# Batch 3's x through the array's quarters, and batch 2's x later in its output stage with the first two tiles of the next h side by side

## The chip, the cores and the metric

One core of a Trainium2 chip. The metric is the device time of the core in microseconds. The profile's span is about 1.9 us shorter than it in most executions.

## The reference

Linear attention for 8 batches and 8 heads, then a two-layer MLP with an exact Gelu:

```python
q_s = softmax(q, axis=-1)          # (8, 8, 576, 64)
k_s = softmax(k, axis=2)           # over the sequence
kv  = einsum('bhsd,bhse->bhde', k_s, v)
attn = einsum('bhsd,bhde->bhse', q_s, kv)
x = attn.transpose(0, 2, 1, 3).reshape(4608, 512)
h = x @ w_in                       # 512 x 2048
out = (0.5 * h * (1 + erf(h / sqrt(2)))) @ w_out
```

## The kernel before

The kernel treats 512 of the 576 rows of each batch as one chunk (`M`), and the 8 x 64 remaining rows as a ninth. For a chunk, the h stage (`h_phase`) makes 16 tiles of h with 4 matmuls each, and ScalarE puts Gelu on each; the output stage (`y_phase`) makes 4 tiles of the output with 16 matmuls each. The attention of the next batches is threaded into these two stages: functions are called after a given tile `t`, or after matmul `(j, t)` of the output stage.

x of a batch is made by four matmuls, one for each pair of heads, with a block-diagonal 128x128 of kv as weights (`x_step`), and a copy (the evacuation) takes each product out of PSUM. Half of each block is zeros. For batches from `QB` on, the two heads of every second pair are swapped, so that the four 64x64 blocks of two pairs fall on the four quarters of the array, and eight 64x64 matmuls take the place of four whole ones (`x_quad`). The swap is made in the exponentials, in four activations rather than one.

```python
QB = 4
...
def exp_heads(b, dst, src):
    if b < QB:
        nc.scalar.activation(out=dst, in_=src, func=AF.Exp)
        return
    for s, u in ((0, 0), (1, 1), (2, 3), (3, 2)):
        nc.scalar.activation(out=dst[:, s::4], in_=src[:, u::4], func=AF.Exp)
...
def x_quad(b, engs="vvvv"):
    st[b]["xT"] = attn_sb.tile([128, HP, M], BF16, tag="xT", name="xT")
    for hp in range(HP):
        pool, tag = (psum_a, "a") if hp < 2 else (psum_y, "y")   # psum_y: the output stage's
        st[b][f"x{hp}"] = pool.tile([128, M], FP32, tag=tag, name="ps")
    for half in range(2):
        for r in range(2):
            for i in range(2):
                hp = 2 * half + i
                pr = slice(r * 64, r * 64 + 64)
                c = slice((r ^ i) * 64, (r ^ i) * 64 + 64)
                nc.tensor.matmul(
                    st[b][f"x{hp}"][c, :], kvbd[b][pr, hp, c], st[b]["qT"][pr, :, hp, :],
                    start=True, stop=True,
                )
    for hp in range(HP):
        x_evac(b, hp, engs[hp])
...
def h_phase(c, ins, groups={}, pre={}):      # groups={0: 2}: tiles 0 and 1 side by side
    ...
        for dm in range(NDM):
            for ps, t in zip(pss, ts):
                nc.tensor.matmul(
                    ps, wi_bf[:, dm, t * 128:(t + 1) * 128], xT[:, dm, :],
                    start=(dm == 0), stop=(dm == NDM - 1),
                )
...
load(3)                                      # q, k, v of batch 3
exp_q(2, parts=2); exp_k(2); exp_q(3); exp_k(3)
table(AF.Gelu)
y_phase(1, {
    (0, 15): [lambda: norm_q(2, 0, 2)],
    (1, 1): [lambda: norm_q(2, 1, 2, nc.vector)],
    (1, 12): [lambda: kv_step(2, (0, 1))],
    (2, 2): [lambda: kv_step(2, (2, 3))],
    (1, 15): [lambda: xbar_step(2)],         # DMA transpose of q: qT
    (3, 3): [lambda: x_step(2, 0)],
    (3, 6): [lambda: x_step(2, 1)],
    (3, 9): [lambda: x_step(2, 2)],
    (3, 12): [lambda: x_step(2, 3)],
})
```

The softmax here doesn't subtract the row's maximum and nothing guards it: scores larger than these inputs give would overflow.

## Time and profile before

| | kernel before |
|---|---|
| time, first three runs | 287.24 us median (287.09 to 288.22) |
| span of the profiled execution | 286.5 us |
| TensorE / ScalarE / VectorE / GpSimd busy | 97 / 55 / 42 / 13% |
| "the stretch": start of batch 1's output stage to start of batch 2's h stage | 62.20 to 79.14: 16.94 us |
| batch 2's h stage | 79.14 to 94.95: 15.81 us |
| VectorE's last copy ends; the span ends | 283.17; 286.5 |

In the profile's lines PE is TensorE, DVE VectorE, ACT ScalarE, POOL GpSimd and SP SyncE; SPq and ACTq are the queues on which SyncE and ScalarE issue DMAs. L323 is a line of the kernel: L323 x as whole matmuls, L346 x as quarters, L376 h, L386 the output. A bracket gives the idle time before an instruction, and what ended it.

Read it from the top: TensorE bounds the kernel, and the two stages that the change touches follow each other on TensorE.

### The profile page before, as it was taken

The page shows a single profiled execution, that of the slowest core. Times are in us where ns is not written, and L with a number is a line of the kernel's source. Part 1 is how long each engine was busy: PE and PEld are TensorE (multiplying, and loading weights), DVE is VectorE, ACT ScalarE, POOL GpSimd, SP SyncE. Part 2 cuts the span into 40 slices and gives each one's busy share as a digit, 9 for nine tenths or more (in the row PEclk, how much of TensorE's full clock was granted, in tenths as well). Part 3 has the DMA queues.
Part 4 walks back from the last instruction along what each step waited for, and adds up shares of the span by engine and source line. Part 5 has one row for each costly group of instructions (what it writes and reads, how often), then busy time and mean ns, then how long its engine had stood idle before and what let it go on. Part 6 is the DMA issues. An engine that isn't in the chain of part 4 may idle for free.

```text
span 286.5 us, 3845 instructions
## 1 busy us (share of the span) xinstructions
PE 278.7 (97%) x1507; PEld 131.3 (46%) x1507; DVE 120.2 (42%) x240; ACT 157.1 (55%) x251; POOL 38.5 (13%) x34
## 2 busy tenths in 40 slices
PE   8989999999899999999999999999999999999994
PEld 3534454445345445444544454445444444444443
DVE  7564387128595555345422632363235112110012
ACT  5777684779355843685268625771665165017400
POOL 5730032002020050005000400041002200000000
PEclk9999999999999999999999999999999999999999
DMA  7999999999809929932995189716701600120033
GB/s 233 375 383 385 373 388 296 293 283 244 161 37 251 297 97 233 258 115 76 214 266 146 73 190 264 172 73 160 136 0 72 147 2 0 73 76 0 0 73 76
DMA packets 58465, 50.05 MB, mean 175 GB/s; under 512 B 26576, under 2 KB 48336, under 8 KB 58448
## 3 DMA queue, kind: packets, MB, share of 16 engines
q1 hardware_dynamic: 58288, 49.68, 62.4%
q8 instruction: 12, 0.20, 0.3%
q10 hardware_dynamic: 160, 0.13, 0.1%
q14 instruction: 5, 0.04, 0.0%
HBM read 36.70 MB, written 9.44 MB: 161 GB/s over the span
## 4 chain that ended last, share of the span: by engine, by line
PE 77%; DMA 15%; SPq 2%; DVE 2%; ACT 1%; issue 1%; POOL 0%; ACTq 0%
PE ps L376 39%; PE ps L386 33%; DMA f<-in_v_dram 7%; DMA f<-in_q_dram 4%; DMA w<-in_moe_w_in_dram 3%; DMA qT<-e 2%; PE ps L251 2%; SPq L108 1%; PE ps L408 1%; DVE qsum L241 1%; PE ps L323 1%; PE ps L346 1%; SPq L117 1%; ACT L145 0%; SPq L463 0%
## 5 line engine op out<-in xcount | busy, mean ns | idle before, releaser
L381 ACT ACTIVATE g<-ps 128x512 bf16<-128x512 f32 x144 | 85.7, 597 | 100.0 <-PE ps L376 100.0
L376 PE MATMUL ps<-xT,wi_bf 128*128 128x512 bf16 x576 | 129.9, 379 | 1.0 <-POOL wi_bf L452 0.8
L386 PE MATMUL ps<-wo_bf,g 128*128 128x512 bf16 x560 | 124.0, 379 | 0.0
L376 PEld LDWEIGHTS <-wi_bf 128*128 128x128 bf16 x576 | 55.2, 98 | 66.5 <-issue 2.4
L386 PEld LDWEIGHTS <-g 128*128 128x128 bf16 x560 | 54.6, 98 | 65.8 <-issue 1.0
L393 DVE COPY y_sb<-ps 128x512 f32<-128x512 f32 x35 | 23.8, 686 | 73.2 <-PE ps L386 73.0
L243 POOL TENSOR_TENSOR e<-e,recq 128x1024 bf16<-128x1024 bf16 (+1 forms) x10 | 27.5, 2758 | 176.8 <-DVE recq L242 94.5
L356 DVE CAST xT<-ps 128x512 bf16<-128x512 f32 x33 | 21.6, 687 | 34.7 <-PE ps L346 20.8
L241 DVE TENSOR_REDUCE qsum<-e 128x16 f32<-128x1024 bf16 (+1 forms) x13 | 21.1, 1623 | 6.9 <-ACT e L145 6.7
L224 DVE CAST v_aug<-f 128x512 bf16<-128x512 f32 x24 | 10.3, 429 | 10.2 <-DMA f<-in_v_dram 9.6
L97 ACT ACT_TABLE_LOAD x9 | 11.5, 1283 | 0.9 <-PEq L659 0.7
L273 DVE TENSOR_SCALAR kvbd<-ps,rec 64x64 bf16<-64x64 f32 x48 | 11.6, 281 | 0.7
L476 PE MATMUL ps<-kvbd 128*128 128x512 bf16 x35 | 10.4, 467 | 1.2 <-DVE scr L85 1.2
L145 ACT ACTIVATE e<-f 128x1024 bf16<-128x1024 f32 (+1 forms) x7 | 8.1, 1174 | 4.9 <-DMA f<-in_q_dram 4.9
L182 ACT ACTIVATE ek<-f 64x1152 bf16<-64x1152 f32 x8 | 9.3, 1162 | 2.6 <-DMA f<-in_k_dram 2.5
L148 ACT ACTIVATE e<-f 128x512 bf16<-128x512 f32 x16 | 8.8, 618 | 0.0
L148 ACT ACTIVATE ek<-f 128x512 bf16<-128x512 f32 x16 | 8.7, 614 | 0.0
L251 PEld LDWEIGHTS <-ek 128*128 128x128 bf16 x96 | 6.8, 97 | 3.2 <-ACT ek L145 0.6
L251 PE MATMUL ps<-v_aug,ek 128*128 128x129 bf16 x96 | 8.1, 220 | 0.1
L467 DVE CAST wo_bf<-w 128x2048 bf16<-128x2048 f32 (+1 forms) x5 | 5.1, 1014 | 5.8 <-DMA w<-in_moe_w_out_dram 5.7
L323 PE MATMUL ps<-qT,kvbd 128*128 128x512 bf16 x16 | 6.1, 381 | 1.3 <-DMA qT<-e 0.7
L476 PEld LDWEIGHTS <-kvbd 128*128 128x128 bf16 x35 | 3.9, 116 | 6.7 <-issue 3.3
(53 smaller groups left out, 99.0 us busy)
## 6 DMA issues: line engine op xcount, KB each, us to landing
out_dram<-y_sb SPq DMA_DIRECT2D x32, 256.0 KB, 2.4
f<-in_q_dram SPq DMA_DIRECT2D x6, 1024.0 KB, 8.3
f<-in_k_dram SPq DMA_DIRECT2D x6, 1024.0 KB, 11.7
f<-in_v_dram SPq DMA_DIRECT2D x6, 1024.0 KB, 10.1
w<-in_moe_w_in_dram SPq DMA_DIRECT2D x6, 512.0 KB, 8.3
w<-in_moe_w_out_dram SPq DMA_DIRECT2D x3, 1024.0 KB, 12.1
f<-in_k_dram SPq DMA_DIRECT2D x4, 576.0 KB, 9.1
f<-in_v_dram SPq DMA_DIRECT2D x8, 288.0 KB, 9.4
```

The lines of the kernel that those rows point to most:

```text
L97: nc.scalar.activation(out=scr[:, 1:2], in_=scr[:, 0:1], func=func)
L148: nc.scalar.activation(out=dst[:, s::4], in_=src[:, u::4], func=AF.Exp)
L241: nc.vector.reduce_sum(out=qsum, in_=eq[:, :, hs, :], axis=AX.X)
L243: eng.tensor_tensor(out=eq[:, :, hs, :], in0=eq[:, :, hs, :], in1=recq.unsqueeze(3).to_broadcast([128, J, w, D]), op=ALU.mult,)
L251: nc.tensor.matmul(ps, st[b]["ek"][:, j, hs, :].rearrange("p h d -> p (h d)"), v_aug[b % 2][:, j, hp, 0:PW], start=(j == 0), stop=False,)
L273: nc.vector.tensor_scalar_mul(out=kvbd[b][pr, hps[i], c * 64:c * 64 + 64], in0=ps[pr, i, c * (D + 1):c * (D + 1) + D], scalar1=rec[pr, i:i ...
L356: nc.vector.tensor_copy(out=st[b]["xT"][:, hp, :], in_=ps)
L376: nc.tensor.matmul(ps, wi_bf[:, dm, t * 128:(t + 1) * 128], xT[:, dm, :], start=(dm == 0), stop=(dm == NDM - 1),)
L381: nc.scalar.activation(out=g[:, t, :], in_=ps, func=AF.Gelu)
L386: nc.tensor.matmul(ps, st[c]["g"][:, t, j * 128:(j + 1) * 128], wo_bf[:, t, :], start=(t == 0), stop=(t == NDF - 1),)
L393: nc.vector.tensor_copy(out=y_sb, in_=ps)
L476: nc.tensor.matmul(ps, zeros[:, 0:128], zeros, start=True, stop=True)
```

## The change

Its intent: keep TensorE from standing still for batch 2's transposed q (qT), with enough distance from x to h to hide x's last copy; and make batch 3's x at the price of two matmuls rather than four.

```diff
-    QB = 4
+    QB = 3
...  (exponentials of the ninth chunk: batch 3's heads swapped too, ten activations instead of five)
-        (3, 3): [lambda: x_step(2, 0)],
-        (3, 6): [lambda: x_step(2, 1)],
-        (3, 9): [lambda: x_step(2, 2)],
-        (3, 12): [lambda: x_step(2, 3)],
+        (3, 6): [lambda: x_step(2, 0)],
+        (3, 8): [lambda: x_step(2, 1)],
+        (3, 10): [lambda: x_step(2, 2)],
+        (3, 12): [lambda: x_step(2, 3, "s")],
...
         if QB <= b < B:
-            s[9] = [lambda: x_quad(b)]
+            s[12 if late else 9] = [lambda: x_quad(b)]
...
-        h_phase(c, ins)
+        h_phase(c, ins, groups={0: 2} if c == 2 else {})
```

`"s"` puts the last copy of x on ScalarE. `late` is true for batch 3.

More of the change, by code (lines that the diff above doesn't have):

```diff
@@ L157, in exp_main @@
             f = st[b][name + "f"]
-            nc.scalar.activation(out=e[:, 0:QB // 2], in_=f[:, 0:QB // 2], func=AF.Exp)
-            for s, u in ((0, 0), (1, 1), (2, 3), (3, 2)):
-                nc.scalar.activation(
-                    out=e[:, QB // 2:, s::4], in_=f[:, QB // 2:, u::4], func=AF.Exp
-                )
+            nc.scalar.activation(out=e[:, 0], in_=f[:, 0], func=AF.Exp)
+            exp_heads(2, e[0:R, 1], f[0:R, 1])
+            exp_heads(3, e[R:128, 1], f[R:128, 1])
+            exp_heads(4, e[:, 2:4].rearrange("p j h d -> p h j d"),
+                      f[:, 2:4].rearrange("p j h d -> p h j d"))
             return
```

## The prediction

> **What bounds the kernel now.** I read the page first: which engine is busy, then what it waits for.
>
> ```profile
> PE 278.7 (97%) x1507; PEld 131.3 (46%) x1507; DVE 120.2 (42%) x240; ACT 157.1 (55%) x251; POOL 38.5 (13%) x34
> ...
> PEclk9999999999999999999999999999999999999999
> ```
>
> TensorE is busy for 278.7 of 286.5 us, at full clock from end to end. No other engine passes 55%. Busy alone proves little here, so the second view is the list of what TensorE waited for over the whole span; this is all of it:
>
> ```profile
> engine line waited for: us in total, times, longest us
> PE ps L476 <- DVE scr L85: 1.2, 1, 1.2
> PE ps L376 <- POOL wi_bf L452: 0.8, 1, 0.8
> PE ps L323 <- DMA qT<-e: 0.7, 1, 0.7
> PE ps L197 <- DVE v_aug L188: 0.4, 1, 0.4
> PE ps L323 <- ACT kvbd L210: 0.3, 1, 0.3
> PE ps L323 <- DVE kvbd L212: 0.2, 1, 0.2
> ```
>
> Six waits, 3.6 us in all. Four of the six lie in the start-up or in batches 0 and 1 (their lines belong to the first two batches' own code), a fifth is the warm-up's. Only the third, 0.7 us for the transposed q (qT), lies where the change reaches. The reader should take from this that there are two ways to shorten the kernel: remove a TensorE wait, or give TensorE less to do. Shortening VectorE or ScalarE work cannot pay.
>
> The third view, TensorE's instructions in order of time, places that wait (start, duration, then the instructions of one kind in a row):
>
> ```profile
> 71.13 3.83 PE L386 MATMUL ps<-wo_bf,g 128*128 128x512 bf16 x17
> 75.69 0.38 PE L323 MATMUL ps<-qT,kvbd 128*128 128x512 bf16 x1 [0.73 <-DMA qT<-e]
> 75.91 0.81 PE L386 MATMUL ps<-wo_bf,g 128*128 128x512 bf16 x3
> ```
>
> This is batch 2's first x matmul, inside the last quarter of batch 1's output stage. TensorE is in order, so it stands from 74.96 to 75.69 us. The chain that ended last tells why qT comes then:
>
> ```profile
> 65.40 1.23 DVE qsum L241
> ...
> 68.90 1.24 DVE e L243
> ...
> 70.29 5.36 DMA qT<-e
> ...
> 75.69 0.38 PE ps L323
> ...
> 79.31 7.77 PE ps L376 x36
> ```
>
> The exponentials of q follow the last Gelu of the stage before (62.4 us), then come the row sums, the normalisation, and a DMA transpose of 5.36 us. Nothing in that chain waits for a TensorE instruction that the change moves, so qT stays at about 75.69 us. After this wait TensorE has none until the end.
>
> **What the Trainium skill says.** "Perfetto Trace Analysis", in Tensor Engine Instruction, says that a matmul's reported end is an estimate. The trace agrees: a 128x512 matmul is shown as 379 ns, yet 64 of them take 13.81 us on the chain, 0.2158 us each. I therefore count by starts. "TensorE: Matmul & The Clock Gate", in Back-to-back issue gap, gives N/2.4 + 2.5 ns, thus 216 ns for N = 512, which is this figure; the 131 ns which the same section gives for a stream of weight load and matmul pairs is not what this trace has. "TensorEngine Tiling (Array Packing)", in Key Properties, says that different tiles of the array run in parallel, and that changing the tiling mode drains it. Both are seen in the trace (next part). "Perfetto Trace Analysis", in DMA Instruction — HWDGE, says that the data movement is not in the DMA instruction's own window. So it is here: the transpose shows 3.34 us on its queue, and lands after 5.36 us.
>
> **The change, part by part.**
>
> *1. Batch 2's x moves from (3,3), (3,6), (3,9), (3,12) to (3,6), (3,8), (3,10), (3,12).* The instruction order confirms it: three more output matmuls come ahead of the first x, and two rather than three between the next. Nothing is added or removed on TensorE. It stopped at 74.96 us; three matmuls of 0.216 us take it to 75.61, where it meets qT at 75.69. So the wait falls from 0.73 to 0.08 us: 0.65 us gained, all of it on TensorE, which sets the end.
>
> *2. Its last evacuation goes to ScalarE, and the first two h tiles run side by side.* This is there to pay for part 1. From 75.69 us, four x matmuls and 9 output matmuls (three pairs and the last three) come before h: 13 x 0.216 = 2.81 us, so h would start at 78.50. Its start is shown at 79.14 before; the 0.64 us agrees with part 1 within rounding. The last x starts 4 matmuls earlier, at 77.64. An evacuation began 0.42 us after its matmul's start (75.69 to 76.11), so ScalarE starts at 78.06; the same copy took 0.586 us in batches 0 and 1, thus 78.65. In the new order its reader is the seventh matmul of h, at 78.50 + 6 x 0.216 = 79.80: 1.1 us to spare. Even without pairing, the fourth matmul would come at 79.15, with 0.5 us left. So I expect the pairing to remove no wait which would else be there: it is worth about zero. It also uses only two of the three PSUM buffers of h, and ScalarE's Gelu (597 ns a tile, against four matmuls or 0.86 us) catches up in a few tiles.
>
> *3. Batch 3's x: eight 64x64 matmuls rather than four 128x128.* Batches 4 to 7 already do this, so the cost is in the trace before:
>
> ```profile
> 118.32 0.38 PE L376 MATMUL ps<-xT,wi_bf 128*128 128x512 bf16 x1
> 118.63 0.41 PE L346 MATMUL ps<-qT,kvbd 64*64 64x512 bf16 x4
> 118.87 0.39 PE L346 MATMUL ps<-qT,kvbd 64*64 64x512 bf16 x4
> 119.19 0.39 PE L376 MATMUL ps<-xT,wi_bf 128*128 128x512 bf16 x1
> ```
>
> (These lines come from narrow looks at the same place; each is one row of four at a time, or one matmul.) Four start within some 0.02 us of each other, the next four 0.24 later. Entering the mode took 0.31 rather than 0.216 us, leaving it 0.32: the drains, some 0.1 us each. From the last h matmul ahead to the first behind it is 0.87 us. Four whole matmuls would have made that 5 x 0.216 = 1.08. The gain is 0.21 us, not the 0.43 that halving would give. A whole-stage check is independent of it: batch 2's h stage, with four whole matmuls, runs from 79.31 to 95.12 (15.81 us); the next, with the quarters, from 108.93 to 124.54 (15.61). Both hold the same 64 h matmuls and the same kv steps, and the difference is 0.20.
>
> *4. ScalarE pays for permuted heads.* q, k and k's rest of batch 3 are each four activations now. In batch 4's stage four 128x512 ones span 2.19 us for q and 2.17 for k, against 1.89 for one 128x2048; four 64x128 span 0.89 against 0.61. Together 0.30 + 0.28 + 0.28 = 0.86 us more. ScalarE finished at 74.27 before, and will at 75.1; it has nothing due until 78.06. For the last batch's q, about ten instructions in place of five (an estimate from the 0.3 us or so that each of the small ones takes, 1.32/4: 1.3 us more); its transpose starts at 224.36, lands some 4.7 us later (median) and is read at 234.2. Some 5 us are free. None of part 4 is on the path.
>
> Sum on the path: 0.65 + 0.21 + 0 + 0 = 0.86 us. 287.24 - 0.86 = 286.4 us, or 0.3%.
>
> **The rivals.**
>
> *A new wait for the PSUM buffers that the quarters borrow.* Two of the four x tiles come from the pool of the output stage, and here, unlike in batches 4 to 7, only three h tiles (12 matmuls, 2.59 us) are left behind them before that stage wants one back. In batch 4 VectorE began 0.45 us after the quarters' start, and did four evacuations in 2.48, so the third is done at about 2.3 us, while the output stage asks at 0.56 + 0.11 + 2.59 = 3.3 us. VectorE is free before it (the kv scaling ends at 90.3, the first x is at 91.5). For: the slack is only 1 us. Against: it is positive by two measured durations. If it failed: up to 0.7 us lost, thus about 287.1.
>
> *qT of batch 3 becomes the wait.* With TensorE 0.65 us earlier, the quarters come at 90.85. Its transpose was issued at 84.94 and lands 4.8 us on (the shorter of the two in this stretch), at 89.74. Even if that stayed put, 1.1 us are left, and it should move with the rest, since its VectorE work follows the last output copy of the stage. Unlikely; a few tenths of a microsecond at most.
>
> *The wait for batch 2's qT is smaller or larger in ordinary runs.* It ends with a DMA whose length depends on other transfers (4.4 to 5.4 us over seven). This one is the longest. Were it 4.7 elsewhere, there would be hardly any wait to remove, and the gain would be 0.21 us: 287.0. Were it longer, the later place would save the same 0.65 and leave the rest. This is the largest uncertainty of the sum.
>
> *ScalarE becomes late.* It would need 3 us more than 74.27 to matter, and gets 0.86. The profile speaks against it.
>
> **Range and chances.** The sum gives 286.4. Below it there is little: only the rest of the wait and noise. Above it, a lost part 1 gives 287.0. The three runs of before spread from 287.09 to 288.22, so their median may itself be off by some tenths. I take 285.8 to 287.2. 2% is 5.7 us; the whole sum of waits in reach is under 1. Faster by over 2%: 0.01. Slower by over 2%: 0.01; that needs a stall which none of the slacks above allows. Within: 0.98.
>
> **What would show it.** Part 1: TensorE's wait for qT falls to 0.1 us or less, and the h stage of batch 2 starts near 78.5 us. Part 2: no TensorE wait for xT at that start, and none would be there without pairing. Part 3: the h stage of batch 2 lasts 15.6 us, with a drain of 0.1 us on both sides of the eight. Part 4: ScalarE ends its exponentials near 75.1 us. Every later stage keeps its length and moves by 0.86. The prediction is wrong if TensorE gains a wait at the start of batch 2's output stage, if qT moves, or if the time rises.

## The result, and the profile after

The kernel after takes 286.94 us (median of 6 runs, 286.12 to 287.47), the kernel before in the same rounds 287.94 us (6 runs, 287.09 to 288.39). The ratio is 0.9969, with a 95% interval of 0.9947 to 0.9992. A ratio is here always the mean time of one kernel's runs over that of the other's of the same rounds, so it is not quite the ratio of the medians. 286.4 was predicted, with a range of 285.8 to 287.2.

The list of what TensorE waited for, kernel after, has as its last two lines:

```profile
PE ps L323 <- DVE kvbd L212: 0.2, 1, 0.2
PE ps L323 <- DMA qT<-e: 0.2, 1, 0.2
```

The wait for qT went from 0.73 to 0.21 us (0.1 or less was said). TensorE's instructions in order of time, kernel after:

```profile
62.09 6.42 PE L386 MATMUL ps<-wo_bf,g 128*128 128x512 bf16 x28
...
75.70 0.38 PE L323 MATMUL ps<-qT,kvbd 128*128 128x512 bf16 x1 [0.21 <-DMA qT<-e]
...
78.50 7.93 PE L376 MATMUL ps<-xT,wi_bf 128*128 128x512 bf16 x35
...
90.95 0.63 PE L346 MATMUL ps<-qT,kvbd 64*64 64x512 bf16 x8
91.51 2.76 PE L376 MATMUL ps<-xT,wi_bf 128*128 128x512 bf16 x11
94.11 13.98 PE L386 MATMUL ps<-wo_bf,g 128*128 128x512 bf16 x63
```

The stretch is now 78.50 - 62.09 = 16.41 us (16.94 before), and the h stage 94.11 - 78.50 = 15.61 (15.81 before). (Counts of 28, 35, 11 and 63 where the program has 29, 36, 12 and 64 are records missing from the trace.) ScalarE in order of time, kernel after:

```profile
74.78 0.20 ACT L97 ACTIVATE scr<-scr 128x1 f32<-128x1 f32 x1
78.06 0.59 ACT L358 CAST xT<-ps 128x512 bf16<-128x512 f32 x1 [3.07 <-PE ps L323]
80.21 1.68 ACT L381 ACTIVATE g<-ps 128x512 bf16<-128x512 f32 x3 [1.57 <-PE ps L376]
```

ScalarE is through with its longer exponentials at 74.98 us, stands idle for 3 us, and makes the copy at 78.06, as worked out. So by the two profiled executions nearly everything fits: 0.53 us from the stretch, 0.20 from the h stage, 0.11 because the second execution reached batch 1's output stage that much earlier. That is 0.84 of the 0.9 us between the spans (286.45 and 285.54 before rounding).

That would be the end, if one execution of each kernel stood for all of them. The spans of the kernel before range over 2.6 us (284.6 to 287.2 in the next round of runs), three times the gain.

### The profile page after: what moved, and what is told of

The parts are those of the page before. It is cut to its first block, busy times and chain, and to the rows that moved or that the text cites. A ratio compares the mean times of both kernels' runs of the same rounds, so it can differ in the third digit from the quotient of the medians.

```text
span 285.5 us, 3838 instructions
## 1 busy us (share of the span) xinstructions
PE 277.1 (97%) x1484; PEld 131.0 (46%) x1511; DVE 119.6 (42%) x239; ACT 159.5 (56%) x266; POOL 38.6 (14%) x34
## 4 chain that ended last, share of the span: by engine, by line
PE 87%; DMA 5%; DVE 2%; ACT 1%; SPq 1%; issue 1%; POOL 0%; ACTq 0%
PE ps L376 43%; PE ps L386 38%; DMA f<-in_v_dram 3%; DMA qT<-e 2%; PE ps L251 2%; PE ps L408 1%; PE ps L346 1%; PE ps L323 1%; DVE qsum L241 1%; SPq L117 1%; PE ps L197 1%; DVE xT L356 0%; ACT L145 0%; DVE e L243 0%; PE ps L255 0%
## 5 line engine op out<-in xcount | busy, mean ns | idle before, releaser
L376 PE MATMUL ps<-xT,wi_bf 128*128 128x512 bf16 x560 | 128.6, 379 | 1.8 <-DVE kvbd L212 0.8
L356 DVE CAST xT<-ps 128x512 bf16<-128x512 f32 x32 | 20.6, 686 | 33.3 <-PE ps L346 22.5
L148 ACT ACTIVATE e<-f 128x512 bf16<-128x512 f32 (+2 forms) x28 | 13.2, 540 | 0.1
L148 ACT ACTIVATE ek<-f 128x512 bf16<-128x512 f32 x20 | 10.9, 614 | 0.0
L145 ACT ACTIVATE e<-f 128x1024 bf16<-128x1024 f32 (+1 forms) x7 | 6.8, 991 | 4.9 <-DMA f<-in_q_dram 4.8
L216 DVE CAST vr_aug<-f 64x512 bf16<-64x512 f32 x6 | 2.5, 416 | 8.1 <-DMA f<-in_v_dram 8.1
```

The costliest lines, as they stand in the source:

```text
L356: nc.vector.tensor_copy(out=st[b]["xT"][:, hp, :], in_=ps)
L376: nc.tensor.matmul(ps, wi_bf[:, dm, t * 128:(t + 1) * 128], xT[:, dm, :], start=(dm == 0), stop=(dm == NDM - 1),)
```

## The experiments

Twelve runs followed, all correct (two of them repeat a kernel unchanged). The first four shared one chip and eleven runs of the kernel before (288.24 us median, 286.60 to 289.16); the last four another eleven (287.75, 286.91 to 289.64). The four between ran once each, beside one run of the kernel before, for their traces: single times that differ by 1 us say nothing here.

### 1. The parts apart

a_move_only is the kernel before with the four new places and nothing else:

```diff
-        (3, 3) ... (3, 6) ... (3, 9) ... (3, 12): [lambda: x_step(2, 3)],
+        (3, 6) ... (3, 8) ... (3, 10) ... (3, 12): [lambda: x_step(2, 3)],
```

> The kernel before with batch 2's four x matmuls moved to (3,6), (3,8), (3,10), (3,12) and nothing else: all four copies on VectorE, no pairing, batch 3 whole. If the move alone carries part 1 (my theory): TensorE's wait for qT falls from 0.73 us to 0.3 or less, no wait for xT appears at the start of batch 2's h stage, the stretch from the start of batch 1's output stage to the start of batch 2's h stage shrinks from 16.94 us to about 16.4, and the h stage stays at 15.81. Time about 0.5 to 0.65 us below before (ratio 0.998). If the pairing or ScalarE's copy is needed for the gain (rival): a wait of 0.4 us or more for xT at that start, and the stretch to the end of the h stage is no shorter than before.

b_quad_only is the kernel after with the four old places, all copies on VectorE, and no pairing:

```diff
-        (3, 6) ... (3, 8) ... (3, 10) ... (3, 12): [lambda: x_step(2, 3, "s")],
+        (3, 3) ... (3, 6) ... (3, 9) ... (3, 12): [lambda: x_step(2, 3)],
-        h_phase(c, ins, groups={0: 2} if c == 2 else {})
+        h_phase(c, ins)
```

> The change without the move, ScalarE's copy and the pairing: batch 3's x through the quarters after h tile 12, batch 2's x where it was. Theory: the wait for qT stays at 0.6 to 0.8 us, the h stage of batch 2 takes 15.61 us instead of 15.81, ScalarE's exponentials end 0.8 us later with nothing waiting for them; time 0.2 us below before (ratio 0.999). Rival (borrowed PSUM buffers or the longer exponentials cost something): h stage plus start of the output stage no shorter than before, or a TensorE wait for a VectorE xT copy.

c_no_pair is the kernel after without the pairing (the second pair of lines alone):

> The kernel after without the pairing of the first two h tiles. Theory (pairing worth nothing at these places): the h stage of batch 2 starts at the same distance from batch 1's output stage as in the kernel after (16.41 us) and lasts 15.61 us, no wait for xT; time within 0.1 us of after. Rival (pairing hides the last copy): a wait of 0.2 us or more for the xT of ScalarE in the fourth matmul of the stage, and the h stage is longer by it.

after_again is the kernel after, unchanged:

> The kernel after, unchanged, for comparison on the same chip. Ratio to before 0.997 (0.7 to 1.0 us), wait for qT 0.1 to 0.3 us, h stage 15.61 us; the gains of a_move_only and b_quad_only in stage lengths should add up to its own. If they do not add, the parts interact and my sum is wrong.

| | time, median of 6 | ratio to before (95%) | wait for qT | stretch | h stage |
|---|---|---|---|---|---|
| a_move_only | 288.32 | 1.0015 (0.9983 to 1.0047) | none | 16.05 | 15.81 |
| b_quad_only | 286.75 | 0.9965 (0.9932 to 0.9997) | none | 16.05 | 15.61 |
| c_no_pair | 286.79 | 0.9970 (0.9933 to 1.0007) | none | 16.04 | 15.61 |
| after_again | 286.70 | 0.9957 (0.9927 to 0.9987) | none | 16.05 | 15.61 |

The h stage does what was said, in each of them. Pairing is worth nothing at these places, as said. But b_quad_only broke my theory: x is at its old place (3,3), and there is no wait for qT. TensorE in order of time, b_quad_only:

```profile
70.64 3.83 PE L386 MATMUL ps<-wo_bf,g 128*128 128x512 bf16 x16
74.31 0.38 PE L323 MATMUL ps<-qT,kvbd 128*128 128x512 bf16 x1
```

A stretch of 16.05 us is one without any wait; all four have it, at either place. So 16.94 and 16.41 in the first two traces were the exceptions. And a_move_only, which should have gained, was no faster than before (its interval includes 1), while b_quad_only gained about as much as the whole change (0.9965 against 0.9957, the intervals overlap): I had expected neither. after_again's wait, 0.1 to 0.3 us by its expectation, was missing too.

Why is qT on time here? Its transpose lands sooner. The DMA issues of 60 to 76 us, kernel before (first trace; out<-in, queue, count, KB, us to landing):

```profile
f<-in_v_dram SPq DMA_DIRECT2D x1, 1024.0 KB, 10.2
out_dram<-y_sb SPq DMA_DIRECT2D x3, 256.0 KB, 2.8
f<-in_v_dram SPq DMA_DIRECT2D x1, 128.0 KB, 11.6
qT<-e SPq DMA_TRANSPOSE x1, 5.4
```

and b_quad_only:

```profile
f<-in_v_dram SPq DMA_DIRECT2D x1, 1024.0 KB, 10.2
out_dram<-y_sb SPq DMA_DIRECT2D x3, 256.0 KB, 2.5
f<-in_v_dram SPq DMA_DIRECT2D x1, 128.0 KB, 11.4
qT<-e SPq DMA_TRANSPOSE x1, 4.3
```

The 1 MB load is batch 3's v. It was issued at 62.97 us in the first and landed at 73.20, 2.9 us after the transpose's issue; in b_quad_only at 61.11 and 71.35, only 1.6 us after it. New theory: how long that load lies beside the transpose sets the transpose's length, and with it whether there is a wait at all.

### 2. The overlap, free and forced

before_again is the kernel before, unchanged, one look:

> The kernel before, unchanged, profiled a second time. New theory, from the four runs just seen: the wait for qT that my part 1 was to remove is not there in every execution. It appears when batch 3's last load (v) lands after about 73 us, with the transpose (issued at about 70 us) beside it; then the transpose takes 5.4 us. When v lands at about 71 us the transpose takes 4.4 us and there is no wait even in the old place. So here: either transpose 4.3 to 4.5 us, v landed before 71.5 us, wait for qT 0.2 us or less; or transpose 5.2 us or more, v landed after 72.5 us, wait 0.5 us or more. Rival (the wait belongs to the kernel, whatever the transfers do): wait 0.6 to 0.8 us with a short transpose.

l_v_ahead_before issues the big v load right ahead of the transpose, m_v_ahead_after does the same in the kernel after, and k_v_behind_before issues it right behind. The small load of v's rest stays where it was:

```diff
-    load(3)
+    load_main(3, "q", q)
+    load_both(3, "k", k)
+    load_both_r(3, "v", v)          # v's last 64 rows
...
+        (1, 14): [lambda: load_both_f(3, "v", v)],                               # l, m
         (1, 15): [lambda: xbar_step(2)],
or
-        (1, 15): [lambda: xbar_step(2)],
+        (1, 15): [lambda: xbar_step(2), lambda: load_both_f(3, "v", v)],         # k
```

> The kernel before with batch 3's big v load (1 MB) issued between the first output copy and the transpose, so that the two always overlap. Theory (the overlap sets the transpose's length): transpose 5.2 us or more, wait for qT 0.5 us or more at the old place (3,3), in any execution. Rival (transpose length has another cause): 4.3 to 4.5 us and no wait.

> The kernel after with the same forced overlap. Theory: the transpose is as long as in l_v_ahead_before, and the wait for qT is smaller than there by three output matmuls, 0.65 us (or is gone); the stretch from the start of batch 1's output stage to the start of batch 2's h stage is shorter by that. Rival (the later place only moves the wait elsewhere): the stretch is as long as in l_v_ahead_before.

> The kernel before with batch 3's big v load issued right behind the transpose, so nothing of that load runs beside it. Theory: transpose 4.4 us or less, no wait for qT at the old place, stretch from the start of batch 1's output stage to batch 2's h stage about 16.2 us rather than 16.94. The v load then lands at about 79 to 82 us, before its casts at 84.7, so no new wait. Rival (queue order does not matter): transpose over 5 us and a wait of 0.5 us or more.

TensorE's first x of batch 2 in before_again, l_v_ahead_before and m_v_ahead_after, from the same view of each (L335 is the same source line, moved by the edit):

```profile
74.42 0.38 PE L323 MATMUL ps<-qT,kvbd 128*128 128x512 bf16 x1
```

```profile
75.36 0.38 PE L335 MATMUL ps<-qT,kvbd 128*128 128x512 bf16 x1 [1.17 <-DMA qT<-e]
```

```profile
75.39 0.38 PE L335 MATMUL ps<-qT,kvbd 128*128 128x512 bf16 x1 [0.60 <-DMA qT<-e]
```

All traces, ordered by how long v was still on its way when the transpose was issued (v's landing less the transpose's issue):

| trace | first x at | v lands after the transpose's issue by | transpose | wait for qT | stretch |
|---|---|---|---|---|---|
| k_v_behind_before | (3,3) | (issued behind it) | 4.4 | none | 16.05 |
| a_move_only | (3,6) | 0.5 | 4.4 | none | 16.05 |
| o_less_pe_after (below) | (3,6) | 1.5 | 4.4 | none | 16.05 |
| after_again | (3,6) | 1.5 | 4.4 | none | 16.05 |
| b_quad_only | (3,3) | 1.6 | 4.3 | none | 16.05 |
| before_again | (3,3) | 1.7 | 4.4 | none | 16.05 |
| c_no_pair | (3,6) | 1.7 | 4.4 | none | 16.04 |
| n_more_pe_before (below) | (3,3) | 1.7 | 4.3 | none | 16.05 |
| p_tight_ends (below) | (3,9) | 2.6 | 5.1 | none | 16.05 |
| j_batch2_quad (below) | (3,10) | 2.9 | 5.3 | none | see there |
| before | (3,3) | 2.9 | 5.4 | 0.73 | 16.94 |
| after | (3,6) | 3.0 | 5.5 | 0.21 | 16.41 |
| l_v_ahead_before | (3,3) | 4.1 | 5.8 | 1.17 | 17.37 |
| m_v_ahead_after | (3,6) | 4.1 | 5.9 | 0.60 | 16.81 |

The two go together in every row, and three of the traces set the order by hand. Up to 1.7 us of overlap the transpose takes 4.3 to 4.4 us and TensorE does not wait, at either place; from 2.6 us on it takes 5.1 to 5.9. Forcing the overlap brings the wait back, and with the load behind the transpose there is none. There the load was issued at 71.97 us, before the transpose landed at 74.40, so my expectation that nothing of it runs beside the transpose was not quite met: in these traces the load that lengthens the transpose is one issued ahead of it. Why v's load comes later in some executions than in others was not looked into. Where there is a wait, the later place is worth 0.53 us (before against after) and 0.56 us (l against m) of the stretch. I had said 0.65, the three matmuls; the transposes of the two later-place traces were 0.1 us longer, which is about the rest. before_again met its first alternative, except that v landed at 71.63 us, just past the 71.5 that I had set. k and m also met their expectations for the stretch (m lost 0.56 us rather than 0.65), but k's time was no better than before (288.92 us). The other single times were 288.71 (before_again), 288.00 (l), 287.17 (m) and 287.83 us (the kernel before beside them).

The time of k, like those of a_move_only and before_again, made me look at the end of the trace.

### 3. The end of the program

In before_again VectorE's last copy ends at 281.62 + 0.29 = 281.91 us, 1.3 us sooner than in the first trace of the same kernel (283.17). Yet its span is 286.8 us, not 285.2. What the queue that issues the stores waited for in the last 10 us (us in total, times, longest), before_again:

```profile
SPq L670 <- DMA out_dram<-y_sb: 3.3, 2, 3.0
```

and after_again:

```profile
SPq L670 <- DMA out_dram<-y_sb: 1.7, 2, 1.3
```

The last output writes land later. The DMA issues of the last 10 us, before_again:

```profile
out_dram<-y_sb ACTq DMA_DIRECT2D x1, 96.0 KB, 4.1
out_dram<-y_sb SPq DMA_DIRECT2D x1, 32.0 KB, 3.6
out_dram<-y_sb ACTq DMA_DIRECT2D x1, 32.0 KB, 3.8
```

and after_again:

```profile
out_dram<-y_sb ACTq DMA_DIRECT2D x1, 96.0 KB, 2.4
out_dram<-y_sb SPq DMA_DIRECT2D x1, 32.0 KB, 2.0
out_dram<-y_sb ACTq DMA_DIRECT2D x1, 32.0 KB, 2.1
```

So the span ends 4.9 us after the last copy in before_again (5.0 in k_v_behind_before, 4.6 in a_move_only), and 3.2 or 3.3 us after it in all other traces. What else moves there? One packet of the instruction queue, 16,384 bytes. The Trainium skill, "Runtime: NRT & Kernel Launch", Instruction fetch mechanics, says that an engine's program is refilled in blocks of 16 KiB, 256 instructions, over a DMA queue of its own. The trace agrees in size: this queue moves 12 such packets in every trace, room for 3,072 instructions, and TensorE's program has 1507 weight loads and as many matmuls, 3014 together (with 1511 of each, 3022; the expectations below write 3016 and 3024). That the queue is TensorE's is inferred from this. The time at which the last one starts, less the end of VectorE's last copy:

| traces | TensorE's weight loads and matmuls | last fetch | span after the last copy |
|---|---|---|---|
| before_again, k_v_behind_before, a_move_only | 3014 | +1.06 to +1.10 | 4.6 to 5.0 |
| before, l_v_ahead_before (both with a wait for qT) | 3014 | -2.06 to -2.07 | 3.2 to 3.3 |
| after, after_again, b_quad_only, c_no_pair, m_v_ahead_after, p_tight_ends (below) | 3022 | -3.7 to -3.9 | 3.2 |
| j_batch2_quad (below) | 3030 | -4.7 | 3.2 |

In the three long endings, the fetch starts while the last writes are under way (+1 us). In the traces where it comes about 2.06 us ahead of the last copy (o_less_pe_after below is a third) it starts while the two writes before the last are under way, and then these are the late ones: they land after 3.3 to 3.8 us rather than 2.2 to 2.4, and the end does not move. The quarters add 8 instructions to TensorE's program (16 for batch 3's x in place of 8), and with that the last block is fetched earlier. That the length of the program is what counts, rather than the quarters, was a guess. Two runs test it. n_more_pe_before gives the kernel before 4 tiny matmuls more, o_less_pe_after takes 4 of the warm-up's matmuls from the kernel after:

```diff
     warm(30)
+    warm(4, 16)          # n: 4 matmuls of 16 columns
or
-    warm(30)
+    warm(26)             # o
```

> The kernel before with 4 tiny matmuls (16 columns) more in the warm-up, so that TensorE's program has the same 3024 instructions as the kernel after. New theory from the traces: the executions of the old kernel without a wait for qT end late, because TensorE's last instruction fetch (16 KB) starts 1.1 us after VectorE's last copy and lies on the last output write, which then lands after 3.7 to 4.2 us instead of 2.4; in the new kernel, with 8 instructions more on TensorE, that fetch started 3.7 to 3.9 us before the last copy in all five traces. If the length of TensorE's program is what counts: here the fetch comes 2 us or more before the last copy, the last ScalarE-queue write lands after 2.4 us, the span ends 3.2 us after the last copy in place of 4.9, and the median is about 1 us below before (ratio 0.996 to 0.998) without any of the change's parts. Rival (the quarters or ScalarE's extra instructions do it): fetch after the last copy, landing 3.5 us or more, time as before (ratio 0.999 to 1.001). If there is a wait for qT in this trace, the fetch tells nothing new, as in the kernel before.

> The kernel after with 4 warm-up matmuls fewer (26 rather than 30): TensorE's program has the 3016 instructions of the kernel before. Theory (length of the program): the late fetch comes back, at 1 us after the last copy, the last ScalarE-queue write lands after 3.5 us or more, the span ends 4.6 us or more after the last copy, and the gain over before shrinks from 0.997 to about 0.999 to 1.000. Rival (the quarters or ScalarE's program do it): fetch 3 us or more before the last copy, landing 2.4 us, ratio 0.995 to 0.998 as in the kernel after.

n_more_pe_before, the DMA issues of the last 10 us:

```profile
out_dram<-y_sb ACTq DMA_DIRECT2D x1, 96.0 KB, 2.4
```

Its last fetch starts at 278.46 us, 3.84 before the end of the last copy (282.30), and the span ends 3.2 us after it, with no wait for qT (stretch 16.05) and none of the change's parts. In the profile the expectation is met in full. The time is less clear: 287.58 us median, ratio 0.9987 (0.9956 to 1.0019). The means differ by 0.35 us (287.56 against 287.91), where I had expected about 1; the ratio is nearer to the rival's 0.999 than to the 0.996 to 0.998 of my theory, and the interval includes 1. Nor does the timed span show an earlier end: its mean is 285.63 us, and 285.65 in the kernel before. The whole 0.35 us is device time outside the span (1.92 against 2.27 us in the mean).

o_less_pe_after missed. The fetch did move, from -3.7 or more to -2.06 us, but not past the last copy, and the 96 KB write on ScalarE's queue landed after 2.4 us. Its time is between the two, 287.39 us, ratio 0.9976 (0.9944 to 1.0008). So the length of the program moves the fetch, but it is not the only thing that places it: with 3014 of them it was seen at -2.06 and at +1.1. What chooses between these two is open.

One more observation, without a cause that I could show. Device time less span is 1.8 to 2.2 us in most runs, but over 2.3 us (up to 3.25) in 12 of the 34 repeated runs with a recorded span of kernels with 3014 weight loads and matmuls (before 4 of 11 and 3 of 11, a_move_only 1 of 6, o_less_pe_after 4 of 6), and in 0 of 30 with 3022 (after and after_again, b_quad_only, c_no_pair, n_more_pe_before, 6 each). Whatever this is, in these runs it goes with the program's length, not with x's place. On the first chip it makes 0.38 of the 1.24 us between the means of the kernel before and after_again (2.32 against 1.94); the other 0.86 us is span (285.61 against 284.75).

### 4. The slacks of the prediction, used up

p_tight_ends is the kernel after with x of batch 2 as late as it can be, no pairing, and batch 3's quarters as the last thing of the h stage. The two stretches are read apart:

```diff
-        (3, 6) ... (3, 8) ... (3, 10) ... (3, 12): [lambda: x_step(2, 3, "s")],
+        (3, 9) ... (3, 11) ... (3, 13) ... (3, 15): [lambda: x_step(2, 3, "s")],
-            s[12 if late else 9] = [lambda: x_quad(b)]
+            s[15 if late else 9] = [lambda: x_quad(b)]
-        h_phase(c, ins, groups={0: 2} if c == 2 else {})
+        h_phase(c, ins)
```

> The kernel after with three things set so that slacks of my prediction are used up: batch 2's x at (3,9), (3,11), (3,13), (3,15); no pairing of the first h tiles; batch 3's quarters after h tile 15, right ahead of the output stage, instead of 12. By the prediction's numbers: ScalarE's copy of the last x is ready 0.42 + 0.59 + 0.02 = 1.03 us after that matmul's start, the fourth h matmul asks for it at 4 x 0.216 = 0.86, so a TensorE wait of 0.15 to 0.25 us for the xT of ScalarE (which the pairing would hide). And the output stage asks for its PSUM buffer 0.67 us after the start of the quarters, while the third copy ends at 2.3 us: a TensorE wait of 1.5 to 1.8 us for VectorE's xT copy at the start of batch 2's output stage, against none with the quarters at 12. If there is no wait or one under 1 us there, the slack of 1 us that I gave for 12 was mis-sized, or the buffers are not what I think.

TensorE in order of time, p_tight_ends:

```profile
77.21 8.12 PE L376 MATMUL ps<-xT,wi_bf 128*128 128x512 bf16 x36
...
92.44 0.63 PE L346 MATMUL ps<-qT,kvbd 64*64 64x512 bf16 x8
94.83 13.97 PE L386 MATMUL ps<-wo_bf,g 128*128 128x512 bf16 x64 [1.77 <-DVE xT L356]
```

The output stage waits 1.77 us for VectorE's copy out of the buffer that the quarters borrowed; 1.5 to 1.8 was expected. The first nine h tiles take 8.12 us instead of 7.93: 0.19 us lost (0.15 to 0.25 expected), the fourth matmul starting at 78.05 rather than at 77.21 + 3 x 0.216 = 77.86. Both slacks were sized right. The wait in the h stage is too short for a bracket in the timeline and is seen only in the starts; that it is for ScalarE's copy, which ends at 78.00 us, is read from the order of times. The pairing has a use, but only for an x later than the change puts it.

### 5. One step further

j_batch2_quad puts batch 2's x through the quarters too:

```diff
-    QB = 3
+    QB = 2
-        (3, 6) ... (3, 8) ... (3, 10) ... (3, 12): [lambda: x_step(2, 3, "s")],
+        (3, 10): [lambda: x_quad(2, "vsvs")],     # two of its tiles in psum_h
```

> The kernel after with batch 2's x also through the quarters, all eight matmuls after (3,10), copies on VectorE and ScalarE in turn, two of its tiles in the free buffers of h. From the sum that I used: TensorE saves 0.21 us more, so the stretch from the start of batch 1's output stage to batch 2's h stage is 15.85 us without a wait for qT (16.05 for four whole matmuls); ScalarE's exponentials end about 1.2 us later than in the kernel after, at about 76 us, still ahead of its copies. Time 0.2 us below the kernel after: ratio to before 0.995 to 0.997. Rivals: the longer first exponentials delay the transpose by 0.3 us or more and a wait for qT comes back; or the tiles of h are freed late and a wait of 0.2 us or more stands at the start of the h stage.

TensorE in order of time, j_batch2_quad:

```profile
69.12 0.40 PE L249 MATMUL ps<-v_aug,ek 128*128 128x129 bf16 x4 [0.58 <-ACT ek L148]
...
76.55 0.63 PE L344 MATMUL ps<-qT,kvbd 64*64 64x512 bf16 x8
```

The wait for qT did not come back and the h tiles were free, so neither rival was right; but the stretch is 16.68 us (61.52 to 78.20), worse than 16.05. Batch 2's exponentials of k now end at 69.06 us (68.51 in the kernel after, whose stage began 0.57 us later), after eight small activations for q and eight for k, and TensorE stands for them at its kv matmuls, 0.58 us by the bracket. By the stretch, 0.83 us more pass than the 15.85 expected; the bracket leaves a part unexplained. I had checked the end of ScalarE's series, not its middle. The time is 287.40 us (ratio 0.9982, 0.9949 to 1.0015), above after_again's 286.70 on another chip. No version here is shown to beat the kernel after, and b_quad_only and c_no_pair cannot be told from it.

## Why the prediction was right, and where not

The time was within the range, 0.5 us above the point. Part by part:

- **Part 3, the quarters (0.21 us): right**, and the firmest term. The h stage of batch 2 is 15.61 us in place of 15.81 in every trace with the quarters after tile 12 and no wait.
- **Part 2 and the PSUM rival: right.** No wait for xT; without pairing (c_no_pair) nothing changes; p_tight_ends found both slacks where the sums had put them. The rival of batch 3's qT did not come true either: it landed at 89.14 us, 1.8 us before the quarters at 90.95.
- **Part 4: right.** ScalarE ended at 74.98 us; 75.1 was said. The last batch's exponentials went from 2.29 to 3.41 us, 1.1 more. The 1.3 that I wrote is four times 0.33 us, where five more instructions would have been 1.65: near by a slip, and off the path in any case.
- **Part 1 (0.65 us): right in mechanism, wrong in how often.** The step that failed is "so qT stays at about 75.69 us": it took one execution's arrival as the kernel's. In the two profiled executions the gain was 0.53 us, since qT came 0.12 us later in the stage; by starts 0.36 us of waiting were left (16.41 - 16.05), not 0.08. In executions where batch 3's v lands early there is nothing to gain; at the old place, free of any forcing, one trace of four had a wait (before; not before_again, b_quad_only, n_more_pe_before). The third rival named this, with the DMA's 4.4 to 5.4 us in view, but I gave the sum full weight, from an execution that at 288.38 us was slower than all three runs of the median. Of eleven traces with the load left where it was, four had a transpose of 5.1 us or more, so an estimate of what part 1 is worth on average is 4/11 x 0.53, some 0.2 us.
- **A term was missing: the end.** I read the profile up to TensorE's last matmul and took the rest as fixed. With the shorter TensorE program the last writes landed up to 1.8 us late in three of six traces; with 8 instructions more in none of seven. How much of the measured 0.9 to 1.2 us (0.9969 and 0.9957 of some 288) is due to this is not settled: n_more_pe_before, which has it alone, gained 0.35 us, with an interval from 1.3 us gain to 0.5 us loss, and all of it outside the span, so that the late writes of the traces are not what its timed runs show.

So 0.20 us of the gain is shown in every trace, part 1 is shown to be there in some executions and not in others, and a part outside the span goes with the length of TensorE's program. What makes up the rest of the gain in span stays open: the late writes are seen in traces, not in the times. That 0.86 was close to what was measured is in part luck.

## What to carry to other kernels

A wait on a DMA in one trace is a sample: look at what shares the DMA engines with it, compare the profiled execution's own time with the median, and ask for a second trace of the unchanged kernel before crediting its removal. Compare stage lengths between traces (here 16.05 and 15.61 us repeat to 0.01) when the whole times scatter by more than the effect. Where a change adds or removes instructions on the longest program, look at the last microseconds too: the change can act there without touching anything there.

## What the Trainium skill lacked or had wrong

- "TensorE: Matmul & The Clock Gate", Back-to-back issue gap: its 131 ns for a sustained stream of weight loads and N = 512 matmuls is not found here; 64 such pairs take 13.81 us, 216 ns each, its own figure for the single gap.
- "TensorEngine Tiling (Array Packing)", Key Properties: says that a mode switch drains, but not how long. Here some 0.1 us into the mode and 0.1 out of it, so that eight 64x64 matmuls of 512 columns save 0.20 us against four whole ones, not 0.43.
- "DMA: Bandwidth & Descriptors", DMA Transpose (X-bar): no word on how long a transpose takes beside other traffic. The same transpose (16 blocks of 128x128) took 4.3 to 4.4 us with a 1 MB load landing up to 1.7 us after its issue, 5.1 to 5.5 with 2.6 to 3.0 us, and 5.8 to 5.9 with 4.1.
- "Runtime: NRT & Kernel Launch", Instruction fetch mechanics: calls the cost of a block boundary mostly hidden. In three traces the last block's fetch lay beside the last output writes, and these landed after 3.3 to 4.2 us rather than 2.0 to 2.4; in three others it lay beside the two writes before the last, and those landed after 3.3 to 3.8 us. That the fetch is the cause, and what places it (-3.8, -2.06 or +1.1 us from the last copy), the runs do not prove.
- "Perfetto Trace Analysis", Tensor Engine Instruction: that the end is an estimate has a consequence which it does not draw. The 0.73 us of wait shown is counted from an estimated end 0.16 us after the next start would have been; by starts (71.13 + 17 x 0.216 = 74.80 against 75.69) the wait cost 0.89 us, and the stretch agrees (16.94 - 16.05).
